# A pointwise 1x1 layer on one core: dw scales the weight evictions, and the first supertile is written out

## The chip, the core and the metric

The kernel runs on one core of one Trainium2 chip. The metric is the device time of an execution in microseconds (us); lower is better. The core has a matrix engine (TensorE, PE in the profile, with its weight loads as PEld), VectorE (DVE), ScalarE (ACT), GpSimd (POOL) and a queue engine (SyncE, SP). They run side by side and wait for each other through semaphores. TensorE writes its sums to PSUM, which has eight banks for each partition; a bank holds 512 float32 values. VectorE and ScalarE read PSUM and write SBUF, and the DMA engines move data between SBUF and memory.

## The reference

```python
H = W = 384; C = 384; k = 1
# x: (1, 384, 384, 384), dw: (1, 1, 384), pw: (384, 384), all bfloat16
out = x * dw[0, 0][None, None, None, :]
return jnp.einsum('bhwc,cd->bhwd', out, pw)
```

With k = 1 there is no neighbourhood: each of the 147,456 pixels has 384 channels, each channel is scaled by its dw, and the row is multiplied by the 384 x 384 matrix pw. The scale can go into the weights once: out = x @ (dw[:, None] * pw).

## The kernel before, in words

**Tiling.** The pixels are cut into 288 supertiles of 512 pixels. A supertile is computed in 12 steps, one for each pair of a block b (64 channels) and a parity par (`steps`, line 210). A step has four matmuls, q = 0 to 3, each on its own 32 rows of the array and into its own PSUM bank; each contracts 32 channels, for 128 pixels and 384 outputs (`supertile`, lines 212 to 233, matmul at line 222). Supertiles of even number use the PSUM half `PS[0]` and the buffer `Ts[0]`, those of odd number `PS[1]` and `Ts[1]`. After a supertile's last step ScalarE copies its four banks to an output buffer as bfloat16 (line 426), and SP stores that buffer.

**x.** SP loads x in chunks of 1, 1, 1, 1, 2, 4, 5, 5 and then 10 supertiles, into three buffers (`load_x`, line 121). VectorE transposes 32 x 32 blocks of a supertile, as 32-bit words, that is pairs of channels, into `Ts` (`transposes`, line 340). The two channels of a pair lie beside each other then, which is why a step has a parity. The first supertile's first half is transposed in three instructions, one for each block (line 364), and all other halves in one (line 366).

**Weights.** Each quarter of the array needs the same 32 weight rows in its own partitions. They are made on the chip. `sel` is a selection pattern, summed up from an identity matrix (line 387). dw is loaded as one row of 384 values, turned to columns by three small matmuls (line 252) and copied out (line 394). Then three VectorE instructions (line 397) make `sel_w`, one for each third k of pw, as sel times dw. A spread matmul pair (line 272) takes `sel_w` against a third of pw and leaves, in two PSUM banks, two weight blocks that are already scaled and repeated over the four quarters. There are six such pieces, i = 2k + r, over both halves of PSUM. An eviction of both banks at once (`w_out`, lines 379 to 384) copies a piece to `w_r`; VectorE does piece 1 and ScalarE the others (`w_eng`, line 175). The last two pairs are issued twice (`times`, line 262).

**Order at the start.** Each engine runs its instructions in the order of the program. TensorE: 16 matmuls on constants (`idle_work(4)`, line 248), the three small ones for dw, 8 more on constants, the six pieces, and then a loop of 143 turns with supertiles of both halves, and one more supertile. SP: pw's first third, pw's other two thirds, x chunk 0, and then the other chunks and the stores. ScalarE: the load of dw, the table load that its first operation needs, two small copies that also mark both PSUM halves as free (lines 337 and 338), the evictions, and then the output copies. VectorE: sel, dw, the three scaled copies, its eviction, then the transposes of supertiles 0 and 1. In the loop, supertiles of even number wait for the weights at the steps (0, 0), (4, 0) and (4, 1) (`w_first`, line 204), and at blocks 1 and 2 for their transposes (`s_tb`).

**The end.** The last supertile is computed in another form (lines 287 to 314) with a copy of some weights that GpSimd makes (line 330). Nothing of it is changed.

Of the kernel before, what the change touches and what calls it, by code (L numbers as in the profile page):

```python
# [26 lines left out]
def kernel(  # L27
# [45 lines left out]
    raw = consts.tile([P, 3 * (D + 256)], BF16, name="raw")  # L73
    pw_n = raw[:, 0 : 3 * D].rearrange("p (k d) -> p k d", d=D)
    sel_w = raw[:, 3 * D :].rearrange("p (k r q w) -> p k r q w", r=2, q=4, w=32)
# [4 lines left out]
    dw_row = consts.tile([1, C], BF16, name="dw_row")  # L80
    dw_f = consts.tile([P, 3], F32, name="dw_f")
# [31 lines left out]
    with tc.tile_critical(sync_engine=mybir.EngineType.Pool, no_gpsimd_drain=True) as section:  # L113
# [61 lines left out]
        w_eng = [1, 0, 1, 1, 1, 1]  # L175
        w_all = [(s_wr[e], w_eng.count(e)) for e in range(2)]

        nc.scalar.dma_start(dw_row[:], dw.rearrange("a e c -> a (e c)")).then_inc(s_dw, 16)
        nc.sync.dma_start(pw_n[:, 0], pw[0:P, :]).then_inc(s_pw, 16)
        nc.sync.dma_start(pw_n[:, 1:3], pw[P:C, :].rearrange("(k p) d -> p k d", p=P)).then_inc(s_pw2, 16)  # L180
        load_x(0)
# [20 lines left out]
        w_done = [(s_wr[e], w_eng[: i + 1].count(e)) for i, e in enumerate(w_eng)]  # L202

        w_first = {(0, 0): [(0, 1), (1, 3)], (4, 0): [(1, 4)], (4, 1): [(1, 5)]}

        def w_ps(i):
            return PS[0 if i in (2, 3) else 1][:, 2 * (i % 2) : 2 * (i % 2) + 2, :D]
# [4 lines left out]
        def supertile(s, rv):  # L212
            for b, par in steps:
# [22 lines left out]
        def idle_work(n):  # L236
            for _ in range(n):
                for i in range(4):
                    nc.tensor.matmul(  # L239
                        PS[0][:, 2 * (i % 2) + i // 2, :D],  # L240
                        lhsT=ones[32 * i : 32 * i + 32, 0:P],
                        rhs=ones[32 * i : 32 * i + 32, :],
                        start=True,
                        stop=True,
                        tile_position=(32 * i, 0),
                    )

        idle_work(4)

        nc.tensor.wait_ge(s_dw, 16)  # L250
        for k in range(3):
            mm = nc.tensor.matmul(  # L252
                PS[1][:, 0, D + k : D + k + 1],
                lhsT=dw_row[:, P * k : P * k + P],
                rhs=ones[0:1, 0:1],
                start=True,
                stop=True,
            )
        mm.then_inc(s_df)
        idle_work(2)  # L260
        nc.tensor.wait_ge(s_pw, 16)
        times = {(2, 0): 2, (2, 1): 2}
        for k in range(3):
            if k == 1:
                nc.tensor.wait_ge(s_pw2, 16)
            nc.tensor.wait_ge(s_sw, k + 1)
            for r in range(2):
                if k == 2:
                    nc.tensor.wait_ge(*w_done[r])

                for v in [0, 1] * times.get((k, r), 1):
                    mm = nc.tensor.matmul(  # L272
                        PS[(k + 1) % 2][:, 2 * r + v, :D],
                        lhsT=sel_w[64 * v : 64 * v + 64, k, r, :, :].rearrange("p q w -> p (q w)"),
                        rhs=pw_n[64 * v : 64 * v + 64, k, :],
                        start=True,
                        stop=True,
                        tile_position=(64 * v, 0),
                    )
                mm.then_inc(s_w)  # L280
# [56 lines left out]
        for s in range(2):  # L337
            nc.scalar.copy(warm[:, s : s + 1], nc.const_aps.tensor(0.0, [P, 1], F32)).then_inc(s_a[s])  # L338

        def transposes(t, j):  # L340
# [17 lines left out]
            for h in range(2):  # L358
                if h == 0 and j == 0:
                    nc.vector.wait_ge(sem, n)  # L360
                if h == 0 and jj == 0:
                    for b in range(3):
                        x_b = Xw[:, :, 0, 32 * b : 32 * b + 32]
                        nc.vector.transpose(out=Tw[:, b], in_=x_b).then_inc(s_tb if b else s_t[0][0])  # L364
                    continue
# [13 lines left out]
        def w_out(i):  # L379
            e, k, r = w_eng[i], i // 2, i % 2  # L380
            out, in_ = w_r[:, 2 * k : 2 * k + 2, r, :], w_ps(i)
            o = nc.vector.tensor_copy(out, in_) if e == 0 else nc.scalar.copy(out, in_)  # L382
            o._wait_ge(s_w, i + 1)
            o.then_inc(s_wr[e])
# [7 lines left out]
        ).then_inc(s_dwf)  # L392
        nc.vector.wait_ge(s_df, 1)
        nc.vector.tensor_copy(dw_f[:], PS[1][:, 0, D : D + 3]).then_inc(s_dwf)
        nc.vector.wait_ge(s_dwf, 2)
        for k in range(3):
# [80 lines left out]
```

## Time and profile before

| | |
|---|---|
| device time, median of 3 runs | 575.81 us (573.56, 575.96, 575.81) |
| device time of the profiled execution | 573.57 us |
| its span, first to last instruction | 571.8 us |
| granted TensorE clock, mean | 1.000 |
| VectorE busy | 507.7 us (89%) |
| ScalarE busy | 418.7 us (73%) |
| memory read and written | 113.54 and 113.25 MB, 397 GB/s over the span |

A row of a timeline gives the start, the duration, the engine, the line of the program, the operation, what it writes and reads, and in brackets how long the engine was idle before it and what ended that. A row of the view by line or tile gives the shortest, median and longest duration of one instruction in ns, and the first and last start. A row of the view by windows gives a stretch, its length, the busy time of PE, PEld, DVE, ACT and POOL with their counts, the granted clock, the share of time that the 16 DMA engines were busy, and GB/s. A row of the chain gives start, duration and what the chain ran through. The instructions of TensorE overlap, so a matmul's duration is longer than the distance to the next.

### The profile page before, as it was taken

Reading aid. Unit: us, or ns where it says so; the run is one execution under the profiler, and the core shown is the slowest. Engines: PE = TensorE matmul, PEld = TensorE weight load, DVE = VectorE, ACT = ScalarE, POOL = GpSimd, SP = SyncE. Lnnn points to the kernel's source line nnn. Section 1 sums busy time; section 2 is a strip of 40 time slices with the busy share of each in tenths; the row PEclk is TensorE's granted clock in tenths of the full one; section 3 lists DMA queues with packets and bytes.
Section 4 is the critical chain, followed back from the end, with each engine's and each line's share of the span. In section 5 each row is a group of like instructions: output and inputs, shape, how many; then the busy total and the mean of one; then the engine's idle time right before and its main releaser. Section 6 shows DMA issues by size and latency. Waiting matters only on the chain.

```text
span 571.8 us, 29716 instructions
## 1 busy us (share of the span) xinstructions
PE 566.9 (99%) x13843; PEld 414.2 (72%) x13843; DVE 507.7 (89%) x588; ACT 418.7 (73%) x298; POOL 13.9 (2%) x41
## 2 busy tenths in 40 slices
PE   9999999999999999999999999999999999999997
PEld 5777777777777777777777777777777777777775
DVE  7888989989989989989989889889889889889885
ACT  6777777777777777777777777777777777777775
POOL 2042000000000000000000000000000000000000
PEclk9999999999999999999999999999999999999999
DMA  8999999999999999999999999999999999998677
GB/s 317 441 385 385 428 430 432 437 421 414 427 441 422 427 384 422 403 381 392 433 393 383 414 414 406 412 399 420 420 375 435 386 392 397 416 396 361 283 287 260
DMA packets 28085, 226.88 MB, mean 397 GB/s; under 512 B 1450, under 2 KB 7851, under 8 KB 24107
## 3 DMA queue, kind: packets, MB, share of 16 engines
q1 hardware_dynamic: 27140, 225.91, 97.5%
q10 hardware_dynamic: 934, 0.89, 0.4%
q14 instruction: 10, 0.07, 0.0%
q8 instruction: 1, 0.02, 0.0%
HBM read 113.54 MB, written 113.25 MB: 397 GB/s over the span
## 4 chain that ended last, share of the span: by engine, by line
PE 99%; issue 0%; ACT 0%
PE ps L222 98%; PE ps L272 0%; PE ps L239 0%; PE ps L307 0%; PE ps L295 0%; ACT O L421 0%; PE ps L252 0%
## 5 line engine op out<-in xcount | busy, mean ns | idle before, releaser
L222 PE MATMUL ps<-w_r,T 32*128 32x384 bf16 x13776 | 559.8, 321 | 0.1
L366 DVE STREAM_TRANSPOSE T<-X 128x384 uint32<-128x384 uint32 x571 | 499.8, 877 | 55.0 <-PE ps L222 1.1
L222 PEld LDWEIGHTS ps<-w_r,T 32*128 32x128 bf16 x13776 | 411.4, 93 | 148.6 <-issue 0.6
L426 ACT CAST O<-ps 128x1536 bf16<-128x1536 f32 x286 | 411.7, 1440 | 146.4 <-PE ps L222 146.4
L336 POOL COPY Xk<-Xl 32x256 bf16<-32x256 bf16 x16 | 6.3, 396 | 0.0
L335 POOL COPY Xk<-Xl 32x128 bf16<-32x128 bf16 x16 | 4.6, 290 | 25.6 <-DMA Xl<-in_x_dram 24.7
L382 ACT CAST w_r<-ps 128x768 bf16<-128x768 f32 x5 | 3.6, 818 | 0.8 <-PE ps L272 0.8
L330 POOL COPY raw<-w_r 32x768 bf16<-32x768 bf16 x4 | 3.3, 821 | 6.4 <-ACT w_r L382 6.2
L239 PE MATMUL ps<-const-bfloat16-1.0 32*128 32x384 bf16 x24 | 2.2, 516 | 1.1 <-PEq L461 1.1
L272 PE MATMUL ps<-raw 64*128 64x384 bf16 x16 | 2.8, 498 | 0.1
L272 PEld LDWEIGHTS ps<-raw 64*128 64x128 bf16 x16 | 0.8, 114 | 2.2 <-DMA raw<-in_pw_dram 1.2
L338 ACT ACT_TABLE_LOAD x1 | 1.3, 1283 | 1.5 <-PEq L461 1.5
L417 DVE CAST O<-ps 128x384 bf16<-128x384 f32 x2 | 1.0, 552 | 1.4 <-PE ps L222 1.4
L366 DVE STREAM_TRANSPOSE T<-Xl 128x384 uint32<-128x384 uint32 x2 | 1.8, 876 | 0.2
L239 PEld LDWEIGHTS ps<-const-bfloat16-1.0 32*128 32x128 bf16 x24 | 0.7, 117 | 1.5 <-issue 1.5
L387 DVE TENSOR_REDUCE sel<-eye 128x64 f32<-128x128 bf16 x1 | 0.3, 288 | 1.5 <-POOL eye L317 1.5
L349 DVE STREAM_TRANSPOSE T<-Xk 128x384 uint32<-128x384 uint32 x2 | 1.2, 578 | 0.5 <-PE ps L222 0.4
L421 ACT CAST O<-ps 128x384 bf16<-128x384 f32 x2 | 1.0, 479 | 0.7 <-PE ps L307 0.7
L307 PE MATMUL ps<-raw,T 128*128 128x384 bf16 x8 | 1.5, 327 | 0.0
L382 DVE CAST w_r<-ps 128x768 bf16<-128x768 f32 x1 | 1.0, 958 | 0.5 <-PE ps L272 0.5
L364 DVE STREAM_TRANSPOSE T<-X 128x128 uint32<-128x128 uint32 x3 | 0.7, 283 | 0.6 <-DMA X<-in_x_dram 0.6
L421 DVE CAST O<-ps 128x384 bf16<-128x384 f32 x2 | 1.1, 558 | 0.1
(14 smaller groups left out, 5.4 us busy)
## 6 DMA issues: line engine op xcount, KB each, us to landing
X<-in_x_dram SPq DMA_DIRECT2D x25, 3840.0 KB, 22.2
out_dram<-O SPq DMA_DIRECT2D x25, 3840.0 KB, 28.1
X<-in_x_dram SPq DMA_DIRECT2D x3, 1536.0 KB, 18.8
X<-in_x_dram SPq DMA_DIRECT2D x2, 1920.0 KB, 15.7
out_dram<-O SPq DMA_DIRECT2D x2, 1920.0 KB, 24.4
out_dram<-O SPq DMA_DIRECT2D x2, 1536.0 KB, 13.3
X<-in_x_dram SPq DMA_DIRECT2D x6, 384.0 KB, 5.2
out_dram<-O SPq DMA_DIRECT2D x3, 768.0 KB, 6.1
```

The costliest lines, as they stand in the source:

```text
L222: mm = nc.tensor.matmul(PS[s][:, q, :D], lhsT=Ts[s][32 * q : 32 * q + 32, b, par::2], rhs=w_r[32 * q : 32 * q + 32, b, par, :], start=(b, ...
L239: nc.tensor.matmul(PS[0][:, 2 * (i % 2) + i // 2, :D], lhsT=ones[32 * i : 32 * i + 32, 0:P], rhs=ones[32 * i : 32 * i + 32, :], start=True ...
L272: mm = nc.tensor.matmul(PS[(k + 1) % 2][:, 2 * r + v, :D], lhsT=sel_w[64 * v : 64 * v + 64, k, r, :, :].rearrange("p q w -> p (q w)"), rhs ...
L307: mm = nc.tensor.matmul(PS[1][:, m, :D], lhsT=Tk[:, P * (m + 2) : P * (m + 3), par], rhs=w_k[:, par, :], start=False, stop=par == 1,)
L330: nc.gpsimd.tensor_copy(w_k[quads[n]], w_r[quads[n], n]).then_inc(s_wk)
L335: nc.gpsimd.tensor_copy(Xk[quads[n], g:8:4, :], x_b).then_inc(s_xk)
L336: nc.gpsimd.tensor_copy(Xk[quads[n], 8 + g : 24 : 4, :], Xl[quads[g], :, 64 * n : 64 * n + 64]).then_inc(s_xk)
L338: nc.scalar.copy(warm[:, s : s + 1], nc.const_aps.tensor(0.0, [P, 1], F32)).then_inc(s_a[s])
L366: ins = nc.vector.transpose(out=Tw[:, 3 * h : 3 * h + 3], in_=Xw[:, :, j, 96 * h : 96 * h + 96].rearrange("p k (b w) -> p b k w", w=32),)
L382: o = nc.vector.tensor_copy(out, in_) if e == 0 else nc.scalar.copy(out, in_)
L421: o = (nc.scalar.copy if n % 2 else nc.vector.tensor_copy)(Ov[:, n, j, :], PS[s][:, n, :D])
L426: a = nc.scalar.copy(Ov[:, :, j, :], PS[s][:, :, :D])
```

## The change

dw no longer goes into `sel_w`; it is applied when a weight piece leaves PSUM. `sel_w` is made once (one copy). dw is loaded as six rows of 64 values, each four times side by side, and two small matmuls against the identity spread it over the partitions, into `dw_q`. Each eviction takes one bank, is a multiplication by a column of `dw_q`, and runs on ScalarE (eight of them) or VectorE (four). All pieces use `PS[1]`, so a piece waits until the one two before it has been evicted. Pieces 0 to 3 are made ahead of the first supertile. That supertile is written out ahead of the loop; in it, piece 4 is issued ahead of the fifth step and piece 5 ahead of the seventh, and each step waits for its own bank's eviction. VectorE does the eviction (3, 0) between the first and the second transpose of supertile 0, and (5, 1) between the transposes of supertiles 0 and 1. ScalarE's two marking copies come after its first two evictions. x's chunk 0 is loaded by ScalarE's queue. The doubled matmuls are gone, and the matmuls on constants are 16, 4 and 8. The loop now holds an odd and then an even supertile, with a register set ahead of each.

The diff, cut to its core:

```diff
-        w_eng = [1, 0, 1, 1, 1, 1]
-        nc.scalar.dma_start(dw_row[:], dw.rearrange("a e c -> a (e c)")).then_inc(s_dw, 16)
+        w_act = [(0, 0), (0, 1), (2, 0), (2, 1), (3, 1), (4, 0), (4, 1), (5, 0)]
+        w_dve = [(1, 0), (1, 1), (3, 0), (5, 1)]
+        dw_b = dw.rearrange("a e (b c) -> (a e b) c", c=64)
+        nc.scalar.dma_start(dw_n[:], dw_b.unsqueeze(1).to_broadcast([NB, 4, 64])).then_inc(s_dw, 16)
+        load_x(0, nc.scalar)
         nc.sync.dma_start(pw_n[:, 0], pw[0:P, :]).then_inc(s_pw, 16)
         nc.sync.dma_start(pw_n[:, 1:3], pw[P:C, :].rearrange("(k p) d -> p k d", p=P)).then_inc(s_pw2, 16)
-        load_x(0)
...
         def w_ps(i):
-            return PS[0 if i in (2, 3) else 1][:, 2 * (i % 2) : 2 * (i % 2) + 2, :D]
+            return PS[1][:, 2 * (i % 2) : 2 * (i % 2) + 2, :D]
...
+        def w_copy(i):
+            k, r = i // 2, i % 2
+            if i == 2:
+                nc.tensor.wait_ge(s_pw2, 16)
+            if k:
+                for v in range(2):
+                    nc.tensor.wait_ge(*w_ready((i - 2, v)))
+            for v in range(2):
+                mm = nc.tensor.matmul(
+                    w_ps(i)[:, v],
+                    lhsT=sel_w[64 * v : 64 * v + 64, r, :, :].rearrange("p q w -> p (q w)"),
+                    rhs=pw_n[64 * v : 64 * v + 64, k, :],
+                    start=True,
+                    stop=True,
+                    tile_position=(64 * v, 0),
+                )
+            mm.then_inc(s_w)
+
+        def supertile(s, rv, first=False):
+            for n, (b, par) in enumerate(steps):
+                if first and n in (4, 6):
+                    w_copy(n // 2 + 2)
...
-                    if q == 0 and s == 0:
-                        for e, v in w_first.get((b, par), []):
-                            nc.tensor.wait_ge(s_wr[e], v)
+                    if q == 0 and first:
+                        nc.tensor.wait_ge(*w_ready((2 * (b // 2) + par, b % 2)))
...
+        idle_work(1, True)
+        nc.tensor.wait_ge(s_sw, 1)
+        nc.tensor.wait_ge(s_pw, 16)
+        w_copy(0)
+        w_copy(1)
+        nc.tensor.wait_ge(s_dwf, 2)
         idle_work(2)
...
+        w_copy(2)
+        w_copy(3)
+        supertile(0, 1, True)
         with nc.tensor.Fori(0, NS // 2 - 1, 1) as it:
-            rv = nc.tensor.to_reg(it + 1)
-            for s in range(2):
-                supertile(s, rv)
-        supertile(0, NS // 2)
+            supertile(1, nc.tensor.to_reg(it + 1))
+            supertile(0, nc.tensor.to_reg(it + 2))
...
                         nc.vector.transpose(out=Tw[:, b], in_=x_b).then_inc(s_tb if b else s_t[0][0])
+                        if b == 0:
+                            w_out(3, 0)
...
-            o = nc.vector.tensor_copy(out, in_) if e == 0 else nc.scalar.copy(out, in_)
+            eng = nc.vector.tensor_scalar_mul if (i, v) in w_dve else nc.scalar.mul
+            o = eng(w_r[:, b, r, :], w_ps(i)[:, v], dw_q[:, r, b : b + 1])
...
-        for k in range(3):
-            nc.vector.tensor_scalar_mul(
-                sel_w[:, k], sel[:].unsqueeze(2).to_broadcast([P, 2, 4, 32]), dw_f[:, k : k + 1]
-            ).then_inc(s_sw)
-        for i in range(6):
-            w_out(i)
+        nc.scalar.wait_ge(s_dwf, 2)
+        for n, u in enumerate(w_act):
+            if n == 2:
+                for s in range(2):
+                    nc.scalar.copy(warm[:, s : s + 1], nc.const_aps.tensor(0.0, [P, 1], F32)).then_inc(s_a[s])
+            w_out(*u)
+        for u in w_dve[:2]:
+            w_out(*u)
         transposes(*order[0])
+        w_out(*w_dve[3])
         transposes(*order[1])
```

More of the change, by code (lines that the diff above doesn't have):

```diff
@@ L239, in idle_work @@
                     nc.tensor.matmul(
-                        PS[0][:, 2 * (i % 2) + i // 2, :D],
+                        PS[1][:, 2 * (i % 2) + i // 2, :D] if pieces else PS[0][:, i, :D],
                         lhsT=ones[32 * i : 32 * i + 32, 0:P],
@@ L248 @@
         idle_work(4)
+        nc.tensor.wait_ge(s_sel, 1)
         nc.tensor.wait_ge(s_dw, 16)
-        for k in range(3):
+        for par in range(2):
             mm = nc.tensor.matmul(
-                PS[1][:, 0, D + k : D + k + 1],
-                lhsT=dw_row[:, P * k : P * k + P],
-                rhs=ones[0:1, 0:1],
+                PS[0][:, 0, D + NB * par : D + NB * par + NB],
+                lhsT=dw_n[:, :, par::2].rearrange("b q w -> b (q w)"),
+                rhs=eye[0:NB, 0:NB],
                 start=True,
```

53 lines of the change are left out of this document (15 added, 38 removed).

## The prediction

> **What bounds the kernel now.** I read the page's busy times first, then the chain that ended last, then its first 40 us in order of time, then the timelines of the first 8 us engine by engine.
>
> ```profile
> span 571.8 us, 29716 instructions
> PE 566.9 (99%) x13843; PEld 414.2 (72%) x13843; DVE 507.7 (89%) x588; ACT 418.7 (73%) x298; POOL 13.9 (2%) x41
> L222 PE MATMUL ps<-w_r,T 32*128 32x384 bf16 x13776 | 559.8, 321 | 0.1
> ```
>
> TensorE is busy for 99% of the span, and the supertile matmuls (L222) account for 559.8 us with 0.1 us of idle time ahead of them: 287 supertiles of 48 matmuls, 1.95 us each. The chain says where the other 12 us lie; these are its pieces from the start, and below the "..." the long piece that it has from 39.92 us on.
>
> ```profile
> 1.12 1.49 PE ps L239 x13
> ...
> 3.37 1.46 PE ps L272 x8
> 4.83 0.02 issue
> 4.86 1.33 PE ps L272 x8
> 6.19 0.07 issue
> 6.26 33.79 PE ps L222 x825
> ...
> 39.92 526.17 PE ps L222 x12952
> ```
>
> From 6.26 us to 566 us the chain is one run of L222, with no gap in it. Nothing that the change does after the first supertile can be seen in the time unless it opens a gap there. So the question is small: at what time does the first supertile end? Before, it is the stretch 6.26 to 8.21 in the view by windows, all of it TensorE:
>
> ```profile
> 6.26:8.21 1.95, 1.95 (x49) 1.43 (x53) 1.79 (x6) 1.26 (x2) 0.54 (x1) 1.00 1.03 378
> ```
>
> One step of a supertile (four matmuls beside each other) is therefore 1.95/12 = 0.1625 us. What releases the first step at 6.26 is x, by VectorE's timeline and the view of line 364:
>
> ```profile
> 5.81 0.70 DVE L364 STREAM_TRANSPOSE T<-X 128x128 uint32<-128x128 uint32 x3 [0.62 <-DMA X<-in_x_dram]
> L364 DVE STREAM_TRANSPOSE T<-X x3: 269/269/311, 5.8 to 6.2; 128x128 uint32<-128x128 uint32 x3
> 6.05 0.46 DVE L364 STREAM_TRANSPOSE T<-X 128x128 uint32<-128x128 uint32 x2
> 6.43 0.54 DVE L366 STREAM_TRANSPOSE T<-X 128x384 uint32<-128x384 uint32 x1
> ```
>
> VectorE idles 0.62 us for x's first chunk, starts its first transpose at 5.81 and the second at 6.05 (the rows overlap: the second is that of a narrower window), and TensorE starts 0.45 us after the first, that is 0.14 us after its end. Weight work before that (L272) is padded with repeated matmuls and isn't the bound.
>
> **The start of x.** The DMA issues on the queues, then the landing times of the DMA view of the first 3 us, the stretch before the first supertile, and ScalarE's table load:
>
> ```profile
> 0.97 0.39 SPq L179 DMA_DIRECT2D raw<-in_pw_dram  x1
> 0.97 0.53 ACTq L178 DMA_DIRECT2D dw_row<-in_dw_dram  x1
> 1.42 0.41 SPq L180 DMA_DIRECT2D raw<-in_pw_dram  x1
> 1.88 6.61 SPq L133 DMA_DIRECT2D X<-in_x_dram  x9
> ...
> X<-in_x_dram SPq DMA_DIRECT2D x3, 384.0 KB, 4.7
> raw<-in_pw_dram SPq DMA_DIRECT2D x1, 192.0 KB, 2.5
> ...
> 3.30:6.26 2.96, 2.80 (x17) 0.84 (x17) 1.85 (x6) 2.35 (x4) 0.00 (x0) 1.00 1.02 312
> 1.54 1.28 ACT L338 ACT_TABLE_LOAD   x1 [1.54 <-PEq L461]
> ```
>
> x's chunk 0 is issued third on SP, at 1.88. After the change it is second on ScalarE's queue, at 0.97 + 0.53 = 1.50, so 0.38 us sooner, and stands beside pw instead of behind it. SP's chunks 1 and on move up by one issue too. But from 3.30 us on the DMA engines are full (share 1.02, 312 GB/s) and pw's second part has its own 192 KB to bring. Bounds for chunk 0: 0.2 us later (if chunk 1, no longer behind it, takes a share), and 1.0 us earlier (0.38 of issue plus pw's 192 KB at 312 GB/s, 0.62, if it overtook all of them). I take 0.3 us earlier, just under the 0.38, and call the start of the first transpose t = 5.81 - 0.3 = 5.51. The table load moves behind one more issue, to about 2.0 to 3.3, hidden by the wait for pw (below). GpSimd's and SP's other work is only moved past, not lengthened.
>
> **Weight pieces 0 to 3.** The arrival of pw, the spread matmuls, and the evictions, first those of two banks, then one-bank copies from the end of the kernel, which have the shape of the new evictions:
>
> ```profile
> 3.34 0.16 PEld L272 LDWEIGHTS ps<-raw 64*128 64x128 bf16 x4 [0.73 <-DMA raw<-in_pw_dram]
> 3.94 0.20 PEld L272 LDWEIGHTS ps<-raw 64*128 64x128 bf16 x4 [0.44 <-DMA raw<-in_pw_dram]
> L272 PE MATMUL ps<-raw x16: 391/522/524, 3.4 to 5.8; 64*128 64x384 bf16 x16
> ...
> 3.91 3.61 ACT L382 CAST w_r<-ps 128x768 bf16<-128x768 f32 x5 [0.80 <-PE ps L272]
> L382 ACT CAST w_r<-ps x5: 799/817/842, 3.9 to 6.7; 128x768 bf16<-128x768 f32 x5
> ...
> 566.14 0.86 ACT L416 CAST O<-ps 128x384 bf16<-128x384 f32 x2 [0.51 <-PE ps L222]
> L421 ACT CAST O<-ps x2: 479/479/479, 567.5 to 568.2; 128x384 bf16<-128x384 f32 x2
> 566.14 1.02 DVE L417 CAST O<-ps 128x384 bf16<-128x384 f32 x2 [1.37 <-PE ps L222]
> L421 DVE CAST O<-ps x2: 557/558/558, 567.2 to 567.9; 128x384 bf16<-128x384 f32 x2
> ```
>
> A pair of spread matmuls takes 0.52 us, and ScalarE starts 3.91 - 3.37 = 0.54 us after the pair began. A one-bank eviction takes 0.48 us on ScalarE, and a second follows 0.86 - 0.48 = 0.38 us behind the first; on VectorE 0.56 and 1.02 - 0.56 = 0.46. No row shows one with a scale read per partition. Bounds for the spacing on ScalarE: 0.38 (the scale is free) and 0.70 (that of the two-bank evictions, (3.61 - 0.82)/4). I take 0.38, as the bytes are the same.
>
> [...]
>
> Dropping the three scaled copies of sel_w and the doubled matmuls frees VectorE and TensorE before 6 us, but neither set the start: costed at nothing, hidden by the wait for x. pw still arrives at about 3.0 (0.97 plus about 2 us), so pieces 0 and 1 run from 3.05 and are out by about 4.5 (ScalarE: 3.60, 3.98 + 0.48) and 5.0 (VectorE: from 3.93, two at 0.46, 0.56). Piece 2 follows at 4.5, unless pw's second part comes later than that (3.94 before; x beside it could cost up to 0.6); piece 3 at 5.0. Piece 2's evictions on ScalarE end near 5.9. TensorE comes to piece 4, which must wait for them, only at 6.9 (below): 1 us of cover, so a late pw is hidden unless it loses more than that.
>
> **The first supertile, step by step.** Each eviction is now a link of its chain.
> (1) Start: t + 0.45 = 5.96 instead of 6.26: **-0.30**.
> (2) Two spread pairs (pieces 4 and 5) stand between its steps, one step's time each: **+0.33**.
> (3) VectorE does the eviction (3, 0) between x's first and second transpose. Queued behind it are the transposes of blocks 1 and 2 and of the second half, each 0.46 us later than before. Block 1's starts at t + 0.24 + 0.46 = 6.21 (0.24 from 5.81 to 6.05) and, with its 0.27 and 0.14 as above, is of use at 6.62. The third step, which needs it, would have come at 5.96 + 0.325 = 6.29: **+0.33**.
> (4) Piece 4's pair starts two steps later, 6.62 + 0.325 = 6.95. Its evictions on ScalarE are (4,0), (4,1), (5,0), and the last is needed by the eleventh step. Chain: pair 0.39 (the shortest in L272's row), wake 0.04, two spacings 0.76, one eviction 0.48, wake 0.05, together 1.72. TensorE's own work between is 6 steps and two pairs, 8 x 0.1625 = 1.30. The rest is a stall: **+0.42**.
> Its end: 8.21 - 0.30 + 0.33 + 0.33 + 0.42 = 8.99. What is late next: VectorE takes (5, 1) only after piece 5's pair (about 7.8 to 8.4) and chunk 1's transposes come behind that, of use near 8.95, level with the second supertile's start. Before, they had half a microsecond to spare. Later supertiles give VectorE time back (0.88 x 2 of 1.95 us).
>
> **Sum: +0.8 us.** Bounds from the unknowns: x's arrival moves the start by -1.0 to +0.2, but below t = 5.3 it gains nothing, as VectorE's eviction then waits for piece 3 (pair from 5.0, done at 5.55); spacing 0.70 adds 0.64. So about +0.5 to +1.6. The loop that follows has the same 48 matmuls per supertile, and a register set twice per turn instead of once.
>
> The profiled execution took 573.57 us (span 571.80 and 1.77 around it). The runs shown are 573.56, 575.96 and 575.81, so the median (575.81) lies 2.24 above the profile; no row says why. Of the four executions two lie at each height. I place the forecast on their middle, 574.7: **575.5 us**; that is 574.4 if the next runs lie low and 576.6 if they lie high.
>
> **Rivals.**
> (a) The evictions keep up and x gains: without terms 3 and 4 the sum is -0.30 + 0.33, and with x 0.6 earlier -0.3. Against it: term 3 follows from VectorE's order alone. 574.4 on the same base. Chance 0.17.
> (b) x's chunk 0 doesn't gain, or pw's second part suffers from x beside it: term 1 falls to +0.2 or piece 2 slips past its cover, +1.2 to +1.6. For it: DMA share 1.02. 576.0. Chance 0.18.
> (c) Slower: TensorE's fast clock comes late. The row below and that of L272 show matmuls of 384 columns at 522 ns from 1.1 to 5.8 us, against 321 in L222: TensorE worked at about half pace for 4.7 us of nearly closed work.
>
> ```profile
> L239 PE MATMUL ps<-const-bfloat16-1.0 x24: 476/522/523, 1.1 to 2.8; 32*128 32x384 bf16 x24
> ```
>
> The change opens gaps there: about 0.2 us before piece 2, and 0.6 us between piece 3 (done 5.3) and the first step. If such gaps, and the stalls inside the supertile, put the change of pace off until 4.7 us after the first supertile, its 14 units take 0.325 each (4.55 us, end at 10.5, +2.3), and 4.7 us more at half pace lose another 2.35: +4.6, 579.3. It decides from a change of pace at about 12 us (+3); one at 9 us costs +1.7 and stays within 0.5%. Chance 0.06 for over 0.5%. [...]
> (d) The change does nothing that shows, or opens a gap in the loop: setting the register between two supertiles would cost 143 turns x whatever shows; 20 ns give 2.9 us. Against it: the long chain piece has no gap at its loop turns. Chance 0.02 for over 0.5%.
>
> **How the numbers follow.** Forecast 0.57, (a) 0.17, (b) 0.18, (c) 0.06, (d) 0.02. One half per cent of the median, 2.9 us, is about what a measurement of this kernel can tell from no change. Forecast, (a) and (b) lie within it: same 0.90; slower 0.08 from (c) and (d); faster 0.02, for a mechanism that I don't see. Range 573.2 to 577.4: (a) on the low height (573.3) to (b) on the high one (577.4); what is left out is (c), (d) and little else.
>
> **What would show it.** Right: the first transpose near 5.5; VectorE's (3, 0) between the transposes; TensorE idle about 0.3 us at the third step and 0.4 us before the ninth to eleventh; the second supertile from about 9.0; L222 without gaps from there on, and 1.95 us per supertile. Wrong: the second supertile before 8.2; 522 ns matmuls after 6 us; gaps in the loop.

## The result, and the profile after

The change makes the kernel slower: 578.01 us median of 9 runs (576.38 to 578.31) against 573.97 us of 9 runs of the kernel before (573.55 to 575.96). The ratio is 1.0058, with a 95% interval of 1.0042 to 1.0073. The averages lie 3.3 us apart (577.55 against 574.24), as the ratio says; the medians lie 4.0 apart. That is because the times of both kernels lie at two heights: three of the change's nine are 576.4 to 576.7 and six 577.5 to 578.3, and two of the nine of before are 575.8 and 576.0. The profiled execution took 577.50 us with a span of 575.7 us. It lies 3.9 us above that of before in both numbers, so the two profiles show a loss of the size of the medians' difference.

The page after, its busy times and its largest group:

```profile
span 575.7 us, 29725 instructions
PE 569.6 (99%) x13842; PEld 339.7 (59%) x13842; DVE 509.8 (89%) x589; ACT 418.7 (73%) x301; POOL 13.9 (2%) x41
L242 PE MATMUL ps<-w_r,T 32*128 32x384 bf16 x13776 | 562.5, 322 | 0.3 <-DVE T L369 0.3
```

The supertile matmuls (now L242) are still nearly all of it and wait only 0.3 us in all. They are busy 2.7 us longer than before: the matmuls themselves got slower somewhere. The chain of the kernel after, in order of time, from the load of dw on:

```profile
0.97 1.66 DMA dw_n<-in_dw_dram
...
3.24 1.28 ACT L389
...
4.53 1.06 ACT w_r L389 x2
...
5.73 0.84 PE ps L221 x4
6.56 0.02 issue
6.59 0.62 DVE w_r L389
7.21 0.23 DVE T L369
7.43 0.14 issue
7.57 0.83 PE ps L242 x7
8.40 0.43 PE ps L221 x2
8.84 0.76 PE ps L242 x8
9.59 0.43 PE ps L221 x2
10.03 560.00 PE ps L242 x13273
```

Before, the chain ran through TensorE alone from 1.12 us on. Now it goes through dw's load, ScalarE's table load (the 1.28 us at 3.24), two evictions, pieces 2 and 3, VectorE's eviction (3, 0), a transpose, and the supertile with its two pairs. Behind 10.03 us it is one run without a gap, as before.

The stretches of the first three supertiles in the kernel after, by the view by windows (stretch, length, busy PE, PEld, DVE, ACT, POOL, clock, DMA share, GB/s):

```profile
6.48:11.86 5.38, 5.12 (x56) 1.55 (x58) 3.28 (x8) 2.94 (x6) 1.01 (x2) 1.00 1.05 435
11.86:14.12 2.26, 2.26 (x55) 1.29 (x50) 1.97 (x3) 1.44 (x1) 2.14 (x3) 1.00 1.06 447
14.12:16.07 1.95, 1.95 (x55) 1.17 (x50) 1.77 (x3) 1.44 (x1) 0.12 (x1) 1.00 1.01 418
```

The first supertile takes 5.38 us instead of 1.95 and the second 2.26; from the third on it is 1.95. The second starts at 11.86 instead of 8.21, 3.65 us later, and its own 0.31 us make up the 3.96 (the difference of the spans is 3.9). TensorE's weight loads show the pace in the kernel after, one row for a step of four:

```profile
11.86 0.15 PEld L242 LDWEIGHTS ps<-w_r,T 32*128 32x128 bf16 x4 [0.17 <-issue]
12.18 0.15 PEld L242 LDWEIGHTS ps<-w_r,T 32*128 32x128 bf16 x4 [0.17 <-issue]
12.49 7.57 PEld L242 LDWEIGHTS ps<-w_r,T 32*128 32x128 bf16 x188 [0.16 <-issue]
```

A step comes every 0.32 us up to 12.49; from there 188 loads, 47 steps, fit in 7.57 us, 0.16 us each. The profile's clock column reads 1.00 all along, so it doesn't show this; the distance of the steps does. The kept trace has it too: its record of the granted clock, which the views don't print, begins with full speed at 12.47 us. In the kernel before that record begins at 5.93 us, ahead of the first supertile.

What stood still ahead of the first supertile is in ScalarE's and TensorE's timelines of the kernel after, and in its DMA view of the first 3 us:

```profile
3.24 1.28 ACT L389 ACT_TABLE_LOAD   x1 [3.24 <-DVE dw_q L403]
4.53 1.05 ACT L389 ACTIVATE w_r<-ps,dw_q 128x384 bf16<-128x384 f32 x2
```

```profile
3.97 0.83 PE L259 MATMUL ps<-const-bfloat16-1.0 32*128 32x384 bf16 x8
5.73 0.82 PE L221 MATMUL ps<-raw,sel_w 64*128 64x384 bf16 x4 [0.93 <-ACT w_r L389]
```

```profile
5.70 0.26 PEld L221 LDWEIGHTS ps<-raw,sel_w 64*128 64x128 bf16 x4 [1.59 <-DMA raw<-in_pw_dram]
```

```profile
X<-in_x_dram ACTq DMA_DIRECT2D x1, 384.0 KB, 4.1
raw<-in_pw_dram SPq DMA_DIRECT2D x1, 192.0 KB, 4.0
```

The table load waits with the first eviction for dw_q and starts at 3.24, not near 2. Matmuls are missing from 4.80 to 5.73, and again for 0.26 us ahead of the third step at 7.57, which waits for VectorE. pw's second part takes 4.0 us to land instead of 2.5, so it is there at 1.42 + 4.0 = 5.4 (5.46 in the trace), and piece 2 has two gates, 0.2 us apart: the evictions (5.59) and pw. x's chunk 0, issued 0.3 us sooner, takes 4.1 us and lands at 1.6 + 4.1 = 5.7, where it landed before.

### The profile page after: what moved, and what is told of

The parts are those of the page before. It is cut to its first block, busy times and chain, and to the rows that moved or that the text cites. A ratio compares the mean times of both kernels' runs of the same rounds, so it can differ in the third digit from the quotient of the medians.

```text
span 575.7 us, 29725 instructions
## 1 busy us (share of the span) xinstructions
PE 569.6 (99%) x13842; PEld 339.7 (59%) x13842; DVE 509.8 (89%) x589; ACT 418.7 (73%) x301; POOL 13.9 (2%) x41
## 3 DMA queue, kind: packets, MB, share of 16 engines
q10 hardware_dynamic: 1106, 1.28, 0.6%
## 4 chain that ended last, share of the span: by engine, by line
PE 98%; ACT 0%; DMA 0%; DVE 0%; issue 0%; ACTq 0%; POOLq 0%
PE ps L242 98%; PE ps L221 0%; DMA dw_n<-in_dw_dram 0%; PE ps L315 0%; ACT L389 0%; ACT w_r L389 0%; PE ps L303 0%; DVE w_r L389 0%; ACT O L433 0%; DVE T L369 0%; DVE dw_q L403 0%; PE ps L273 0%; PE ps L259 0%; ACTq L484 0%; POOLq L113 0%
## 5 line engine op out<-in xcount | busy, mean ns | idle before, releaser
L242 PE MATMUL ps<-w_r,T 32*128 32x384 bf16 x13776 | 562.5, 322 | 0.3 <-DVE T L369 0.3
L242 PEld LDWEIGHTS ps<-w_r,T 32*128 32x128 bf16 x13776 | 337.3, 93 | 225.0 <-issue 2.5
L389 ACT ACTIVATE w_r<-ps,dw_q 128x384 bf16<-128x384 f32 x8 | 4.2, 577 | 1.8 <-PE ps L221 1.6
L389 DVE TENSOR_SCALAR w_r<-ps,dw_q 128x384 bf16<-128x384 f32 x4 | 2.4, 615 | 3.5 <-PE ps L221 3.5
L221 PE MATMUL ps<-raw,sel_w 64*128 64x384 bf16 x12 | 2.6, 504 | 0.9 <-ACT w_r L389 0.9
L338 POOL COPY raw<-w_r 32x768 bf16<-32x768 bf16 x4 | 3.3, 819 | 9.5 <-DVE w_r L389 9.4
```

Of the source, the lines that this page charges most:

```text
L221: mm = nc.tensor.matmul(w_ps(i)[:, v], lhsT=sel_w[64 * v : 64 * v + 64, r, :, :].rearrange("p q w -> p (q w)"), rhs=pw_n[64 * v : 64 * v + ...
L242: mm = nc.tensor.matmul(PS[s][:, q, :D], lhsT=Ts[s][32 * q : 32 * q + 32, b, par::2], rhs=w_r[32 * q : 32 * q + 32, b, par, :], start=(b, ...
L338: nc.gpsimd.tensor_copy(w_k[quads[n]], w_r[quads[n], n]).then_inc(s_wk)
L389: o = eng(w_r[:, b, r, :], w_ps(i)[:, v], dw_q[:, r, b : b + 1])
```

## The experiments

**Theory A:** TensorE's idle time ahead of the first supertile keeps it at half pace until 12.5 us, and that idle time comes from ScalarE's late table load and from pw's second part, which x now stands beside. **Rival B:** the chain of evictions and transposes alone is longer, and the pace has nothing to do with what lies ahead of the first supertile. The runs of the kernel before beside them had medians of 573.88, 574.00 and 573.97 us.

**e1_load_early.** The changed kernel, with:

```diff
+        for s in range(2):
+            nc.scalar.copy(warm[:, s : s + 1], nc.const_aps.tensor(0.0, [P, 1], F32)).then_inc(s_a[s])
         nc.scalar.wait_ge(s_dwf, 2)
-        for n, u in enumerate(w_act):
-            if n == 2:
-                for s in range(2):
-                    nc.scalar.copy(warm[:, s : s + 1], nc.const_aps.tensor(0.0, [P, 1], F32)).then_inc(s_a[s])
-            w_out(*u)
+        for u in w_act:
+            w_out(*u)
```

> The changed kernel with ScalarE's two marking copies ahead of its wait for dw_q, so that the table load no longer stands behind that wait. Theory A (TensorE's idle time ahead of piece 2, which the table load makes, keeps it at half pace until 12.5 us): the first eviction starts near 3.75 instead of 4.53, piece 2 near 4.8 instead of 5.73, the idle time shrinks from 1.2 us to 0.3, the fast pace comes one window sooner (near 9 us) or earlier, and the time falls by 1.7 us or more, to about 576 or less against 578.0 for the change. Rival B (the loss is the longer chain of evictions alone; the pace has nothing to do with it): the second supertile starts up to 0.8 us sooner, the half pace still ends near 12.5, time about 577.3. Rival C (the table load is not on the chain): no change, 578.

A window has a length of 3.41 us in the clock records of this case's traces (last section): 12.47 - 3.41 = 9.06, and half of 3.41 is 1.7.

577.30 us, ratio 1.0049 (1.0031 to 1.0066): 0.7 us less than the change by the medians, 0.4 by the averages, and the two intervals overlap, so the gain isn't clear of the noise. ScalarE's timeline and the chain of this kernel:

```profile
1.99 1.28 ACT L406 ACT_TABLE_LOAD   x1 [1.99 <-issue]
3.73 1.05 ACT L389 ACTIVATE w_r<-ps,dw_q 128x384 bf16<-128x384 f32 x2 [0.16 <-PE ps L221]
```

```profile
1.42 4.02 DMA raw<-in_pw_dram
...
5.48 0.84 PE ps L221 x4
```

The evictions came 0.8 us sooner, as expected, but piece 2 only 0.25: pw's landing was right behind. The time is the one that rival B gave, yet not for its reason: in this kernel the half pace ends at 10.5 us instead of 12.5. Theory A's numbers for piece 2 missed, because it had left out the second gate. This is what one fix of two gates in a row looks like.

**e2_fill.** The changed kernel, with:

```diff
-        idle_work(2)
+        idle_work(6)
         w_copy(2)
```

> The changed kernel with 16 more matmuls on constants (1.28 us at half pace) between pieces 1 and 2, where TensorE was idle for 1.2 us; nothing else moves, the chain of evictions stays. Theory A (the idle time keeps TensorE slow): the 522 ns matmuls end at 9 us or sooner instead of 12.5, time 575.5 to 576.5. Rival B (the pace depends only on the dense matmuls of the supertiles): half pace until 12.5, time 578.

576.24 us, ratio 1.0039 (1.0029 to 1.0048): 1.8 us less than the change by the medians and 1.2 by the averages, by matmuls whose results nobody reads. The stretches of its first two supertiles, and its matmuls there by line 242:

```profile
6.77:10.64 3.87, 3.15 (x54) 1.05 (x53) 2.73 (x7) 2.89 (x6) 0.28 (x1) 1.00 1.05 431
10.64:12.59 1.95, 1.95 (x53) 1.44 (x52) 1.95 (x4) 1.44 (x1) 1.83 (x3) 1.00 1.05 437
```

```profile
L242 PE MATMUL ps<-w_r,T x104: 317/321/333, 6.8 to 12.8; 32*128 32x384 bf16 x104
```

No matmul of the supertiles takes more than 333 ns, against 522 in the change; the record of the clock begins at 6.67 us. The pace is worth 1.2 us of the second supertile's start (11.86 to 10.64, though the first begins 0.3 us later) and its 0.31. Rival B falls as the whole explanation; the first supertile still takes twice its time at full pace.

**e3_dve_order.** The changed kernel, with:

```diff
                         nc.vector.transpose(out=Tw[:, b], in_=x_b).then_inc(s_tb if b else s_t[0][0])
-                        if b == 0:
-                            w_out(3, 0)
+                    w_out(3, 0)
```

> The changed kernel with VectorE's eviction (3, 0) behind the transposes of blocks 1 and 2 instead of between the first and the second. Both theories: the third step no longer waits 0.45 us, so 0.3 to 0.5 us is gained at half pace, 577.5 to 577.7 against 578.0. If the 0.45 us stop is what keeps the pace down, the 522 ns matmuls end near 9 us instead, and the time falls by about 2 us.

576.86 us, ratio 1.0044 (1.0029 to 1.0058), 1.1 us less than the change by the medians and 0.7 by the averages, where 0.3 to 0.5 were expected. Its profile lies only 0.2 us below the change's span (575.5 against 575.7): pw's second part landed 0.5 us later in it, piece 2 began at 5.99, and the wait at the third step was gone. The half pace still lasted to 12.25. So the gain isn't resolved into its parts.

**e4_before_gaps.** The kernel before, with:

```diff
-        idle_work(2)
         nc.tensor.wait_ge(s_pw, 16)
-        times = {(2, 0): 2, (2, 1): 2}
+        times = {}
```

> The kernel before without the eight matmuls on constants behind dw and without the repeated matmuls of the last two weight pieces: TensorE has idle time near 2.5 to 3.3 and 5.1 to 6.2 us, and every other instruction is as before; the first supertile is still released by x near 6.26. Theory A (idle time before the first supertile keeps TensorE at half pace): the 522 ns matmuls reach into the first supertiles, to 9 us or later, and the time is 1.4 us or more above before, 575.4 or more. Rival B: x is the bound either way, no change, 574.0.

576.13 us, ratio 1.0033 (1.0018 to 1.0048): 2.2 us lost by leaving out 12 matmuls that compute nothing needed. The first supertile's stretch in this kernel:

```profile
6.73:10.49 3.76, 3.76 (x49) 2.12 (x53) 2.08 (x4) 1.26 (x2) 2.23 (x3) 1.00 1.07 434
```

The first supertile runs without a stop (3.76 of 3.76 us busy), but at half pace up to 10.44 us, 1.81 us more than before; the rest, 0.47 us, is its later start (pw's second part landed at 4.5 in this execution). This is theory A with nothing of the change in it. The late pw alone doesn't do it: in e11_before_loop below, which keeps these 12 matmuls, pw landed at 4.33 and the half pace ended at 6.04.

**e5_x_on_sp.** The changed kernel, with:

```diff
-        load_x(0, nc.scalar)
         nc.sync.dma_start(pw_n[:, 0], pw[0:P, :]).then_inc(s_pw, 16)
         nc.sync.dma_start(pw_n[:, 1:3], pw[P:C, :].rearrange("(k p) d -> p k d", p=P)).then_inc(s_pw2, 16)
+        load_x(0)
```

> The changed kernel with x's chunk 0 back on SP, behind pw. Theory A (two gates on piece 2, one behind the other: pw's second part, which x beside it pushes from 3.9 to 5.5 us, and ScalarE's late first evictions at 5.6): pw lands near 3.9 to 4.5 again, x near 5.8 as before, but piece 2 still waits for the evictions, so the second supertile starts at most 0.2 us sooner and the time stays at 577.5 to 578. Rival (pw's landing is the gate): piece 2 starts 1 us sooner and the time falls to 577 or less.

577.77 us, ratio 1.0056 (1.0036 to 1.0075). As expected: pw landed at 4.1, piece 2 still waited for ScalarE and began at 5.53. The average, 577.65, is not below that of the change.

**e6_before_x0act.** The kernel before, with x's chunk 0 on ScalarE's queue:

```diff
+        load_x(0, nc.scalar)
         nc.sync.dma_start(pw_n[:, 0], pw[0:P, :]).then_inc(s_pw, 16)
         nc.sync.dma_start(pw_n[:, 1:3], pw[P:C, :].rearrange("(k p) d -> p k d", p=P)).then_inc(s_pw2, 16)
-        load_x(0)
```

> The kernel before with one part of the change: x's chunk 0 on ScalarE's queue. Theory A (x beside pw pushes pw's second part to 5.5 us and gains nothing itself): pieces 2 to 5 start near 5.5 instead of 3.94, ScalarE's evictions of pieces 2 and 3 end near 7.4, the first supertile starts near 7.4 instead of 6.26, and TensorE's idle time ahead of piece 2 costs the fast pace as well: time 575.0 from the start alone, 576.5 with the pace. Rival (x gains 0.3 us and pw loses nothing that counts): 573.6.

576.68 us, ratio 1.0038 (1.0023 to 1.0053): this part alone loses 2.7 us. Its DMA view of the first 3 us, TensorE's timeline, and the first supertile's stretch:

```profile
X<-in_x_dram ACTq DMA_DIRECT2D x1, 384.0 KB, 4.3
raw<-in_pw_dram SPq DMA_DIRECT2D x1, 192.0 KB, 4.6
```

```profile
6.07 2.10 PE L272 MATMUL ps<-raw 64*128 64x384 bf16 x12 [1.68 <-DMA raw<-in_pw_dram]
```

```profile
8.26:12.00 3.74, 3.74 (x49) 2.14 (x53) 0.86 (x1) 1.26 (x2) 2.21 (x3) 1.00 1.05 440
```

TensorE waits 1.68 us for pw, which costs 2.0 us of the start (8.26 against 6.26; 7.4 was expected, with pw at 5.5 and not at 6.0) and then the pace (3.74 us for the first supertile). x gained nothing: VectorE's first transpose begins at 5.90 here, and at 5.81 before.

**e7_load_xsp.** The changed kernel with the edits of e1_load_early and e5_x_on_sp together.

> The changed kernel with both gates on piece 2 taken away: the marking copies ahead of ScalarE's wait (early table load) and x's chunk 0 back on SP. Theory A: piece 2 starts near 4.8 instead of 5.73, TensorE's longest idle stretch before the first supertile falls from 1.2 to about 0.4 us, the first supertile starts near 6.2 with its third step near 6.9, and the fast pace comes at 9 us or sooner: second supertile near 9.5 to 10, time 575.2 to 575.9. Rival (the rest of the change costs the most, whatever the gates): 577 or more.

576.05 us, ratio 1.0033 (1.0021 to 1.0045). That is 0.15 us above the expected range. One gate alone gave 0.7 and 0.2 us by the medians, neither clear of the noise; both together gave 2.0 by the medians and 1.3 by the averages. Piece 2 began at 4.84, the first supertile at 5.92, 0.3 us sooner than in the kernel before, and still took 4.61 us, three quarters of it at half pace (up to 9.41).

**e8_all_fill.** e7_load_xsp with the edit of e3_dve_order, and:

```diff
-        idle_work(2)
+        idle_work(3)
         w_copy(2)
         w_copy(3)
+        idle_work(2)
```

> The last kernel with VectorE's eviction (3, 0) behind the transposes of blocks 1 and 2, and with 4 more matmuls on constants ahead of piece 2 and 8 behind piece 3, so that TensorE is nearly closed up to the first supertile. Theory A: fast pace by 6 to 7 us, no wait at the third step; what is left is the two spread pairs inside the supertile (0.3 us, and whatever the turn from 64 to 32 rows costs) and ScalarE's three evictions (0.4 to 0.7): second supertile near 9.0, time 574.6 to 575.0. Rival: the time falls below before, 573.8 or less, if ScalarE keeps up.

575.46 us, ratio 1.0016 (1.0005 to 1.0028), 0.5 us above the expected range. In its profile x landed late (6.0) and the half pace still reached into the first three steps.

**e9_pieces_ahead.** e8_all_fill with all pieces made ahead of the first supertile, pieces 2 and 3 in the other half of PSUM as before, the last two pairs twice, and (3, 0) ahead of the transposes. dw still scales the evictions, one bank each:

```diff
-            return PS[1][:, 2 * (i % 2) : 2 * (i % 2) + 2, :D]
+            return PS[0 if i in (2, 3) else 1][:, 2 * (i % 2) : 2 * (i % 2) + 2, :D]
...
-                if first and n in (4, 6):
-                    w_copy(n // 2 + 2)
+                if first and n == 0:
+                    nc.tensor.wait_ge(*w_ready((3, 0)))
+                    nc.tensor.wait_ge(*w_ready((3, 1)))
...
-        idle_work(3)
-        w_copy(2)
-        w_copy(3)
         idle_work(2)
+        for i in range(2, 6):
+            w_copy(i)
```

> The kernel with early table load, x on SP, VectorE's eviction out of the transposes and the filling matmuls, now with all six weight pieces made ahead of the first supertile, in both halves of PSUM as before, the last two pairs issued twice; dw still scales the evictions, one bank each. Theory A (what is left of the loss comes from the two pairs inside the first supertile and the evictions chained to them): the first supertile runs without a stop from about 6.3 to 8.3, time within 0.5 us of before, 574.0 to 574.5. Rival (twelve scaled one-bank evictions are too slow in themselves, 0.48 us apart against 0.70 for two banks): the eleventh step waits, second supertile at 8.8 or later, 574.8 or more.

574.46 us, ratio 1.0007 (0.9998 to 1.0016): not told apart from before. The first supertile's stretch and ScalarE's evictions in this kernel:

```profile
6.84:8.79 1.95, 1.95 (x49) 1.42 (x52) 1.95 (x5) 1.21 (x3) 0.60 (x1) 1.00 1.07 435
```

```profile
5.11 2.94 ACT L388 ACTIVATE w_r<-ps,dw_q 128x384 bf16<-128x384 f32 x6 [0.39 <-PE ps L221]
```

The supertile runs without a stop. The scaled evictions come 0.47 us apart ((2.94 - 0.58)/5), and that is enough. The new form of the eviction isn't in itself what cost the time.

**e10_dve_41.** e8_all_fill with the eviction (4, 1) on VectorE:

```diff
-        w_act = [(0, 0), (0, 1), (2, 0), (2, 1), (3, 1), (4, 0), (4, 1), (5, 0)]
-        w_dve = [(1, 0), (1, 1), (3, 0), (5, 1)]
+        w_act = [(0, 0), (0, 1), (2, 0), (2, 1), (3, 1), (4, 0), (5, 0)]
+        w_dve = [(1, 0), (1, 1), (3, 0), (4, 1), (5, 1)]
```

> The kernel with early table load, x on SP, VectorE's eviction (3, 0) behind the transposes and the filling matmuls, with the eviction (4, 1) on VectorE instead of ScalarE, so that ScalarE has two and not three evictions behind piece 4. Theory A with term 4 of the prediction (ScalarE's three evictions hold the eleventh step): 0.3 to 0.5 us sooner, 575.0. Rival (the slow pace and the pairs hold it, ScalarE keeps up): no change, 575.5.

575.27 us, ratio 1.0018 (1.0007 to 1.0029). Against e8 this tells nothing: 0.2 us, inside both intervals. Its profile happens to be the clean case, at full pace from 4.79 us on. TensorE's timeline there:

```profile
6.02 0.83 PE L242 MATMUL ps<-w_r,T 32*128 32x384 bf16 x16
6.78 0.34 PE L221 MATMUL ps<-raw,sel_w 64*128 64x384 bf16 x2
7.05 0.51 PE L242 MATMUL ps<-w_r,T 32*128 32x384 bf16 x8
7.49 0.34 PE L221 MATMUL ps<-raw,sel_w 64*128 64x384 bf16 x2
7.76 4.95 PE L242 MATMUL ps<-w_r,T 32*128 32x384 bf16 x108
```

Four steps of 0.1625 us would end at 6.67, but the first pair starts at 6.78; the fifth step starts 0.27 us behind the pair, and the second pair repeats this. So a pair costs 0.38 us in all, and the two pairs 0.76. By an estimate that is one step's time, 0.16 us, and about 0.11 us at each turn between 32-row and 64-row matmuls (6.78 - 6.67, and 0.27 - 0.16). The second supertile starts at 9.12, 3.10 us behind the first and not 1.95. Of the rest of the 1.15 us, about 0.09 is a wait of the eleventh step for ScalarE, and 0.28 a wait for x's transposes of the second supertile, which VectorE, now with two evictions in front of them, begins only at 8.41.

**e11_before_loop.** The kernel before, with the first supertile written out and the loop turned, nothing else:

```diff
+        supertile(0, 1, True)
         with nc.tensor.Fori(0, NS // 2 - 1, 1) as it:
-            rv = nc.tensor.to_reg(it + 1)
-            for s in range(2):
-                supertile(s, rv)
-        supertile(0, NS // 2)
+            supertile(1, nc.tensor.to_reg(it + 1))
+            supertile(0, nc.tensor.to_reg(it + 2))
```

> The kernel before with one part of the change alone: the first supertile written out ahead of the loop, and the loop with an odd and then an even supertile and a register set ahead of each; the weights as before. Theory A (nothing behind the first supertile counts): no gap in the loop, same time as before, 573.9 to 574.1. Rival (the register between two supertiles opens gaps): 20 ns per turn show as 2.9 us, 577.

573.83 us, ratio 1.0002 (0.9992 to 1.0011): no difference, and 1.95 us per supertile from 6.56 on. The rival is out, as 2.9 us would have shown.

## Why the prediction was wrong, point by point

**The bound** was read rightly: behind the first supertile nothing counts, and the whole loss lies ahead of 12.5 us (the one run of 560 us, and e11_before_loop). The error is in the first 12 us: +0.8 us were forecast, +4.0 measured by the medians and +3.3 by the averages. The forecast of 575.5 us came nearer to 578.01 than the sum deserved: its base of 574.7, the middle of the two heights, lies 0.7 above the median of before that was then measured.

**The table load**, "to about 2.0 to 3.3, hidden by the wait for pw", is the first step that failed. In the traces it stands directly ahead of ScalarE's first computing instruction (L338 at 1.54 us in the kernel before, L389 at 3.24 in the change, L406 at 1.99 in e1_load_early), and that one now stands behind a wait for dw_q. It ran from 3.24 to 4.52 (dw_q itself was late: dw landed at 2.63, where it had landed before 2.28; whether x beside it has a part in that isn't settled: dw's matmuls began at 2.64 to 2.81 with x beside it, in the change and in e1 to e3, at 2.53 to 2.76 with x back on SP, in e5 and e7 to e10, and at 2.60 in e6_before_x0act, where x is beside it and dw is one row), and the first eviction came at 4.53 instead of 3.60. The order of ScalarE's instructions was in the diff: the marking copies, which carried the load before, had moved behind the evictions.

**pw's second part**, "x beside it could cost up to 0.6", is the second step that failed: it lost 1.5 us (2.5 to 4.0 from issue to landing, and 4.6 in e6_before_x0act), and x, "I take 0.3 us earlier", gained at most 0.1. Over all traces pw's second part took 2.5 to 3.6 us where x's chunk 0 was issued behind it (eight kernels) and 4.0 to 4.6 where it stood on the other queue (five), while x landed at 5.5 to 6.0 and at 5.7 to 5.9. The first step then came at 6.48, behind pieces 2 and 3, and not at 5.96 behind x: term 1 was +0.22 instead of -0.30. Nor was x the only gate before, as the prediction has it: in that trace ScalarE's third eviction, which the first step also needs, ends at 6.12, together with x's first transpose. The share of the DMA engines (1.02) had suggested that x couldn't gain without a loss elsewhere; the prediction saw that and still split the difference in favour of x.

**"A late pw is hidden unless it loses more than that"**: the cover of 1 us was counted for piece 4 alone. Piece 2's lateness also left TensorE without work for 0.93 us, and that has a price of its own: e2_fill, which fills this gap, takes 1.8 us less by the medians.

**"Neither set the start: costed at nothing"**, said of the doubled matmuls among others, is the third step that failed, and the one that cost the most. In these runs the full pace came earlier or later with what fills TensorE ahead of the first supertile (5.93 us in the kernel before and 10.44 in e4_before_gaps, 12.47 in the change and 6.67 in e2_fill). e4_before_gaps shows 2.2 us for the doubled matmuls and the eight on constants together, in a kernel that is otherwise the one before; e2_fill gives 1.8 us back to the change by filling one gap. Rival (c) had this mechanism, with the pace changing "at about 12 us (+3)", and it was given 0.06. What it had too small was the gap ahead of piece 2: "about 0.2 us", where 0.93 was measured.

**Term 2** (two pairs, +0.33) was mis-sized: 0.76 us at full pace in e10_dve_41, and 1.1 at half pace in the change. The 0.22 us by which a pair there takes longer than a step, put down to turning from 32-row to 64-row matmuls and back, were left out. e9_pieces_ahead, with the pairs and the evictions chained to them ahead of the supertile, gains 1.0 us over e8_all_fill.

**Term 3** (VectorE's eviction in front of the second transpose, +0.33) was right in kind: the third step came at 7.57 instead of about 7.12, and without the eviction there it doesn't wait (e3_dve_order). It cost more than itself, as the last section shows. **Term 4** (ScalarE's three evictions, +0.42) didn't show in the change, as the half pace covers it. In e2_fill, at full pace, the chain does run through these three evictions, and TensorE's tenth and eleventh step give their price:

```profile
9.79 0.10 PEld L242 LDWEIGHTS ps<-w_r,T 32*128 32x128 bf16 x4 [0.23 <-ACT w_r L389]
10.26 0.12 PEld L242 LDWEIGHTS ps<-w_r,T 32*128 32x128 bf16 x8 [0.37 <-ACT w_r L389]
```

They lie 0.47 us apart instead of 0.16, a stop of 0.31; e8_all_fill has the same 0.31, and e10_dve_41, with one eviction fewer on ScalarE, about 0.09. So the term was right in kind and near in size. The evictions' spacing is 0.47 to 0.48 us, not the 0.38 taken. Of the two wakes in the term, 0.04 is what the kernel before has from a pair's last matmul to its eviction (3.875 to 3.913), and 0.05 is what the chain of e2_fill has from the eviction to the step (10.22 to 10.26). The kernel after gives the duration of an eviction with its scale as 580 ns, against 479 for the copy before:

```profile
L389 ACT ACTIVATE w_r<-ps,dw_q x8: 572/580/581, 4.5 to 10.1; 128x384 bf16<-128x384 f32 x8
```

That is 0.10 us more with a scale read per partition.

**Where the 4.0 us went.** In the change's own trace the stretch up to the second supertile grew by 3.65 us (11.86 against 8.21). These are three of TensorE's rows in it:

```profile
7.57 0.83 PE L242 MATMUL ps<-w_r,T 32*128 32x384 bf16 x8 [0.26 <-DVE T L369]
8.77 0.82 PE L242 MATMUL ps<-w_r,T 32*128 32x384 bf16 x8
9.96 10.33 PE L242 MATMUL ps<-w_r,T 32*128 32x384 bf16 x220
```

Twelve steps at 0.32 us instead of 0.16 are +1.89, the stop at the third step +0.45, the later start +0.22, and the two pairs +1.1 (8.77 - 7.57 and 9.96 - 8.77, less two steps of 0.32 each). So half of the 3.65 us is a term that the sum doesn't have, the pace. By the runs, the medians first and in brackets the averages of the spans, which leave out what lies around a span: both gates on piece 2 cost 2.0 us together (2.0: 575.8 to 573.8), with part of the pace in it; VectorE's order and the remaining gaps 0.6 (0.6: to 573.2); the pairs inside the supertile and the evictions chained to them 1.0 (0.7: to 572.5); what is left, 0.5 (0.1: to 572.4), can't be told from nothing. No version here beats the kernel before. Its first supertile waits for x and for weights that are ready at the same time, and the earliest first supertile of any run, 5.92 us in e7_load_xsp, is 0.34 us sooner; an estimate of what there was to gain at most is therefore 0.3 us.

## What to carry to other kernels

Before you take out work that "computes nothing" ahead of a dense stretch, look at what pace TensorE runs at there, by the distance between matmuls (a step of four took 0.32 us or 0.16 here), and what keeps it busy until the pace changes. Look for the instruction that carries a one-time cost, such as a table load (1.28 us here), whenever the first instruction of an engine changes or comes to stand behind a wait. A load that was moved to another queue while the DMA engines were full (share 1.02 in the kernel before) took its time here from the load beside it, 4.0 to 4.6 us from issue to landing against 2.5 to 3.6: ask which of them is needed first. When a wait has two gates 0.2 us apart, undo both in one run before concluding that neither matters. And compare the times of many executions where the pace at the start is in play: one profile shows one execution, and nine of the kernel before lay between 573.55 and 575.96 us.

## What the runs showed of the hardware

In these traces the change of TensorE's pace went with the stretch before it, and not only with the number of matmuls. It came at 12.5 us in the change, after the matmul-free stretch at 4.8 to 5.7, and ahead of 6.8 us in e2_fill, where only that stretch was filled. It also varied between nearly equal kernels: in e10_dve_41 no supertile matmul was slow, in e8_all_fill three steps were, with the same matmuls up to there.

The record of the granted clock in the thirteen traces shows a pattern. The full clock was held for 563.20 us in seven of them and for 566.61 in six. The two lengths differ by 3.41 us and are 165 and 166 times 3.413 us, as if the clock changed only at the borders of windows of that length. Counted back in such steps from the beginning of the full clock, the borders lie differently against the start of the program from trace to trace (one is at 2.51 us in the kernel before, at 2.23 in the change, at 0.30 in e1_load_early). This table has, for seven of the traces, when the full clock began, and the time without a matmul in the window that ended there and in the one before it.

| | full clock from, us | without a matmul, last window | the window before |
|---|---|---|---|
| before | 5.93 | 0.09 | 2.02 |
| e2_fill | 6.67 | 0.00 | 1.50 |
| e9_pieces_ahead | 4.29 | 0.30 | 3.41 (no matmul yet) |
| e7_load_xsp | 9.41 | 0.04 | 0.36 |
| e4_before_gaps | 10.44 | 0.00 | 1.07 |
| the change | 12.47 | 0.00 | 0.35 |
| e5_x_on_sp | 12.97 | 0.00 | 0.26 |

In all thirteen the full clock came at the end of a window with at most 0.30 us without matmuls, and no window with 0.35 us or more brought it. In between both happened: 0.25 (e11_before_loop) and 0.30 (e9_pieces_ahead) were little enough, 0.26 (e5_x_on_sp) was not; the ends of matmuls are modelled in a profile, so the limit isn't known more closely. In the change the window from 2.23 to 5.65 has 1.01 us without matmuls, most of it the gap ahead of piece 2, and the next, up to 9.06, has the last 0.08 us of that gap and the 0.26 us in which the third step waited for VectorE. If the time without matmuls decides, as the table suggests, a stop of a quarter of a microsecond kept the half pace for another 3.41 us there, which by an estimate (half of it) costs 1.7; no run has that stop alone. If the borders also lie differently from one execution of a kernel to the next, the same kernel could lose one window more or less. This would make heights like those of the times; only one trace of each kernel is kept, so that isn't shown.

In e10_dve_41, at full pace, a pair on 64 rows between steps on 32 rows took 0.38 us where a step takes 0.16; by the estimate given there that is about 0.11 us for each turn.

What lies around the span was 1.8 us in eight profiled executions, and 2.5 to 2.9 us in those of e1_load_early, e2_fill, e7_load_xsp, e8_all_fill and e10_dve_41 (577.60 against 574.7 in e1_load_early). In these five traces, and in none of the others, one more packet of instructions, of 16 KB, is loaded behind the last instruction. In e1_load_early the DMA view of 575 to 578.5 us counts it, as one packet of kind instruction on queue 8. There it ends at 577.90 us, 0.30 us behind the device time, and in the other four it ends 0.30 to 0.31 us behind theirs. So these times hold 0.7 to 1.1 us that lie behind the last instruction and not in the first 12 us. Between time and span lie 1.7 to 1.8 us in the nine executions of the change, and 1.7 to 2.1 in those of the kernel before. Why some kernels load this packet at the end stays open.
